# A retention layer fused with an ELU MLP on one core: other queues for the first loads, gated v loads, and a respread unit 3

## The chip, the cores and the metric

The kernel runs on one core of a Trainium2 chip. The metric is the device time of one execution in microseconds (us). The kernel before took 319.91 us (median of five runs, 319.39 to 320.42).

## The reference, cut to what matters

```
scores = (q @ k.T) / sqrt(D)                  # B=8, H=8, S=576, D=64
Dmat   = gamma_h ** (i - j) where i >= j, else 0,  gamma_h = 1 - 2**(-5-h)
x      = (scores * Dmat) @ v                  # heads side by side: 4608 tokens x 512
h      = x @ w_in                             # 512 x 2048
g      = h where h > 0, else exp(min(h, 0)) - 1
out    = g @ w_out                            # 2048 x 512
```

All inputs and the output are float32. The kernel's matrix products are in bfloat16.

## The kernel before

The 4608 tokens are 36 units of 128 rows. The decay is split into a factor for the row and one for the column, so that the retention can go unit by unit with a carried state. For each unit the kernel

- loads v (`load_v`, L79: float32, on SP's queue) and q and k (`load_qk`, L88: on GpSimd's queue, POOL, which casts to bfloat16 on the way),
- multiplies v by the column's decay (`scale_v`, L167, on POOL),
- turns q and k to have the head dimension on the partitions (`turn`, L175: eight PE transposes into PSUM, then one copy on DVE, L189, and one on ACT, L190; from unit 12 on a DMA transpose on SP),
- makes the scores (`scores`, L197), masks them (`masks`, L210, DVE), adds the part of the carried state (`inter`, L221), updates the state (`state`, L237), adds the unit's own part (`intra`, L261), and writes the scaled result to the MLP's input (`put_x`, L273, DVE, with the row's decay `gx`, made on ACT by `make_gx`, L160) and the state (`state_out`, L254, ACT).

The units form groups (0 to 2; 3; 4; 5; 6, 7; and so on up to four). `ffn1` (L316) makes one tile of up to 512 hidden values: four matmuls (L326), e = exp(h) on ACT (L331), m = e - 1 on POOL (L333), and later g = min(max(h, 0), m) on DVE (L310), which also frees the PSUM bank. The DVE instruction is put out three tiles behind by `finish` and `tick` (L306 to L314), sooner where the code calls `finish`. Tiles of group 0 and 1 use three banks of the pool `ps_h` in turn, and every fourth tile the one bank of `ps_m`. `ffn2` and `ffn2_half` make the output tiles.

The order on every engine is the order of the program text (`tc.manual_schedule()`). Each engine works its instructions off in that order, and POOL's DMA issues stand in line with its arithmetic. From L484 on a list of slots with due times sets the order. Before that, for units 0 to 6, it is written out by hand, and that is where the change lies:

- L112 to L114: v of units 0 to 3 on SP, q and k of unit 0 on POOL; then the constants (POOL iotas L131 to L136, DVE, ACT), with q and k of unit 1 at L137.
- L396 to L427: dummy matmuls on zeros (`dummy`, L381), the loads of q and k of units 2 and 3 and of w_in and the first half of w_out, and units 0 to 2 one after the other. Dummies stand between their steps.
- L435 to L450: group 0's 16 FFN1 tiles, with unit 3 between them: v scaled after tile 3; turn, second half of w_out, three dummies, scores and mask after tile 7; the rest (`product`) after tile 11, and then the v loads of units 4 to 9. Of these the first waits for a memset on DVE (the argument `after` of `load_v`).
- L451 to L481: group 1's four tiles, the FFN2 halves of units 0 to 3, and units 4 to 6 between them.

Of the kernel before, what the change touches and what calls it, by code (L numbers as in the profile page):

```python
# [9 lines left out]
FP32 = mybir.dt.float32  # L10
BF16 = mybir.dt.bfloat16
# [6 lines left out]
def kernel(  # L18
# [9 lines left out]
    nc = tc.nc  # L28
    PSUM = bass.MemoryType.PSUM

    B, H, S, D = q.shape
    DM, DF = moe_w_in.shape
    P = 128
# [14 lines left out]
    def place(u):  # L48

        pair, r = divmod(u, R)  # L50
        if r < 4:
            return [(0, 2 * pair, P * r, P)]
        if r == 4:
            return [(0, 2 * pair, 4 * P, 64), (64, 2 * pair + 1, 0, 64)]
        return [(0, 2 * pair + 1, 64 + P * (r - 5), P)]
# [5 lines left out]
    qkpool = ctx.enter_context(tc.tile_pool(name="qkpool", bufs=8))  # L61
# [6 lines left out]
    opool = ctx.enter_context(tc.tile_pool(name="opool", bufs=5))  # L68
# [7 lines left out]

    raws, kns = {}, {}

    def load_v(u, after=None):  # L79

        vv = raw.tile([P, H, D], FP32, name="rv", tag="rv")
        if after is not None:
            after.memset(vv[0:1, 0, 0:1], 0.0)
        for p0, b, s0, n in place(u):
            nc.sync.dma_start(vv[p0 : p0 + n], v[b, :, s0 : s0 + n, :].rearrange("h p d -> p h d"))
        raws[u] = vv

    def load_qk(u, *cs):  # L88

        if u not in kns:  # L90
            kns[u] = qkpool.tile([P, 2, H, D], BF16, name="qkn", tag="qkn")
        for c in cs or (0, 1):
            for p0, b, s0, n in place(u):
                nc.gpsimd.dma_start(  # L94
                    kns[u][p0 : p0 + n, c], (q, k)[c][b, :, s0 : s0 + n, :].rearrange("h p d -> p h d")
                )
# [6 lines left out]
    def load_w_in(n):  # L103
        s = slice(n * 512, (n + 1) * 512)
        nc.gpsimd.dma_start(w_in_sb[:, :, s], w_in_v[:, :, s])

    def load_w_out(c, f0, f1):
        s = (slice(None), slice(f0, f1), slice(c * 256, c * 256 + 256))
        nc.gpsimd.dma_start(w_out_sb[s], w_out_v[s])


    for u in range(4):  # L112
        load_v(u)
    load_qk(0)  # L114

    warm = const.tile([P, 512], BF16, name="warm")
    nc.vector.memset(warm, 0.0)  # L117
# [17 lines left out]
    px_i = xpool.tile([P, 2, S - 64], I32, name="px_i", tag="xt").rearrange("p a b -> p (a b)")[:, :S]  # L135
    nc.gpsimd.iota(px_i, pattern=[[1, S]], base=-MID, channel_multiplier=0)  # L136
    load_qk(1)  # L137

    pk = const.tile([P, R], FP32, name="pk")
    nc.vector.tensor_copy(pk, pk_i)  # L140
# [19 lines left out]
    def make_gx(*hps):  # L160
        for hp in hps:
            nc.scalar.activation(gx[:, hp, :S], px, AF.Exp, bias=bx, scale=lgx[:, hp : hp + 1])
# [4 lines left out]
    def scale_v(u):  # L167
        rv = raws[u]
        n = nat.tile([P, H, D], BF16, name="vn", tag="vn")
        nc.gpsimd.tensor_tensor(  # L170
            n, rv, gk[:, u % R].unsqueeze(2).to_broadcast([P, H, D]), ALU.mult
        )
        vns[u] = n

    def turn(u, bank=None):  # L175

        t = tpool.tile([P, 2, HP, P], BF16, name="qkT", tag="qkT")
        n = kns[u]
        if u < PE_TURNED:
            if bank:  # L180
                pool, tag = bank
                ps = [pool.tile([P, HP, P], BF16, name="tr", tag=tag) for c in range(2)]
            else:
                both = ps_s.tile([P, 2, 2, HP, P], BF16, name="tr", tag="sc")
                ps = [both[:, c, 0] for c in range(2)]
            for c in range(2):
                for hp in range(HP):
                    nc.tensor.transpose(ps[c][:, hp], n[:, c, 2 * hp : 2 * hp + 2].rearrange("p h d -> p (h d)"), ident)  # L188
            nc.vector.tensor_copy(t[:, 0], ps[0])  # L189
            nc.scalar.copy(t[:, 1], ps[1])  # L190
        else:
            nc.sync.dma_start_transpose(
                t.rearrange("p c h t -> p (c h) t"), n.rearrange("p c h d -> p (c h d)")
            )
        qkTs[u] = t
# [14 lines left out]
    def masks(u, i=None):  # L210

        if u not in pts:
            pts[u] = ppool.tile([P, 2, HP, P], BF16, name="pt", tag="pt")
        m = mask[:, 1 if u % R == 4 else 0]
        s = slice(0, 2) if i is None else slice(i, i + 1)
        nc.vector.tensor_tensor(  # L216
            pts[u][:, s].rearrange("p i h t -> p (i h) t"), scs[u][:, s].rearrange("p i h t -> p (i h) t"),
            m.unsqueeze(1).to_broadcast([P, (s.stop - s.start) * HP, P]), ALU.mult,
        )

    def inter(u):  # L221

        o = ps_o.tile([P, HP, P], FP32, name="o", tag="o")
        os_[u] = o
        r = u % R
        if r == 0:
            return
        n = 64 if r == 4 else P
        for hp in range(HP):
            for i in range(2):  # L230
                rows = slice(i * D, (i + 1) * D)
                nc.tensor.matmul(  # L232
                    o[rows, hp, :n], sbs[u][rows, hp], qkTs[u][rows, 0, hp, :n],
                    start=(hp == 0), stop=False, skip_group_check=True,
                )
# [70 lines left out]
    def finish(n=0):  # L306

        while late and late[0][0] <= slot[0] - n:
            _, gt_, ph, m, _ = late.pop(0)
            nc.vector.scalar_tensor_tensor(gt_, ph, 0.0, m, ALU.max, ALU.min)  # L310
# [50 lines left out]
    def ffn2_cols(u, c0, c1, bank, copy, queue):  # L361

        g, it = group_of[u]
        pool, tag = bank
        pm = pool.tile([P, c1 - c0], FP32, name="pmh", tag=tag)
        for ft in range(NFT):
            nc.tensor.matmul(  # L367
                pm, gts[g, ft][:, it * P : (it + 1) * P], w_out_sb[:, ft, c0:c1],
                start=(ft == 0), stop=(ft == NFT - 1),
            )  # L370
        ot = opool.tile([P, c1 - c0], FP32, name="oth", tag="ot")
        copy(ot, pm)
        queue.dma_start(out[u * P : (u + 1) * P, c0:c1], ot)

    def ffn2_half(u, c, bank):
        ffn2_cols(u, c * 256, c * 256 + 256, bank, A if u % 2 else V, nc.scalar)


    V, A, G = nc.vector.tensor_copy, nc.scalar.copy, nc.gpsimd.tensor_copy

    def dummy(n, bank=(ps_m, "pm")):  # L381
        dum = bank[0].tile([P, 512], FP32, name="dum", tag=bank[1])
        for _ in range(n):
            nc.tensor.matmul(dum, warm[:, :P], warm, start=True, stop=True)  # L384

    def product(u):
        inter(u)
        state(u)
        intra(u)
        put_x(u)  # L390
        state_out(u)

    h, m = (ps_h, "ph"), (ps_m, "pm")


    dummy(14)  # L396
    load_qk(2)
    make_gx(0, 1)
    turn(0, h)
    load_w_in(0)  # L400
    scale_v(0)
    load_w_in(1)
    scale_v(1)
    load_qk(3)
    dummy(2)
    for u in range(3):
        scores(u)
        inter(u)
        masks(u)
        if u == 0:  # L410
            make_gx(2, 3)
        if u < 2:
            dummy(3)
            turn(u + 1, h)
        else:
            dummy(4)
        state(u)
        intra(u)
        put_x(u)
        state_out(u)  # L420
        dummy(2)
        if u == 0:
            scale_v(2)
            load_w_in(2)
            load_w_in(3)
            load_w_out(0, 0, 8)
            load_w_out(0, 8, 16)  # L427


    def f1(g, n, bank=None):  # L430
        k = 512 // (P * len(GROUPS[g]))
        ffn1(g, k * n, bank)

    o = (ps_o, "o")
    for n in range(16):  # L435
        f1(0, n, m if n % 4 == 3 else None)
        if n == 3:
            scale_v(3)
        if n == 7:
            turn(3)  # L440
            load_w_out(1, 0, 16)
            finish(1)
            dummy(3, o)
            scores(3)
            masks(3)
        if n == 11:
            product(3)
            load_v(4, nc.vector)
            for u in range(5, 10):
                load_v(u)  # L450
    for n in range(4):  # L451
        f1(1, n, m if n == 3 else None)
        if n == 1:
            load_qk(4)
    finish()
    scale_v(4)
    load_qk(5)
    nc.gpsimd.tensor_copy(gx[:, :, S:], gx[:, :, 0:64])
    for u, bank in enumerate((h, h, h, m)):
        ffn2_half(u, 0, bank)  # L460
    scale_v(5)
    load_qk(6)
    ffn2_half(0, 1, h)
    turn(4)
    ffn2_half(1, 1, h)
    scores(4)
    masks(4)
    scale_v(6)
    load_qk(7)
    ffn2_half(2, 1, h)  # L470
    product(4)
    turn(5)
    ffn2_half(3, 1, m)
    scores(5)
    masks(5)
    load_qk(8)
    f1(2, 0)
    f1(2, 1)
    turn(6)
    f1(2, 2)  # L480
    load_qk(9)  # L481


    slots, start, now = [(f1, 2, 3, 1.0)], {}, 1.0  # L484
    for g in range(3, NG + 1):
# [6 lines left out]
        a, b = 0, 2 if g == 4 else 0  # L492
# [33 lines left out]
    for f, g, s, d in slots:  # L526
        while events and events[0][0] <= now + d / 2:
            _, kind, u = events.pop(0)
# [13 lines left out]
    u = NU - 1  # L542
# [31 lines left out]
```

## Time and profile before

| | |
|---|---|
| median of five runs | 319.91 us |
| the profiled execution | 319.93 us, span 317.8 us |
| PE (TensorE matmul) busy | 307.4 us, 97% |
| POOL busy | 201.7 us, 63% |
| DVE busy | 173.5 us, 55% |
| ACT busy | 130.6 us, 41% |
| TensorE clock granted | 1.00 |
| first FFN1 matmul | 19.33 us after the span's start |
| first FFN1 matmul of group 2 | 53.8 us |

The profile is of one execution. Times are in us from the span's start. PE is TensorE's matmuls, DVE is VectorE, ACT is ScalarE, POOL is GpSimd, SP is SyncE. A name such as `SPq` is the sequencer of that engine, which issues DMAs. A row of the timeline has its start, its length, the engine, the line, the operation, what it writes and reads, how many instructions are merged in it, and in brackets how long the engine stood idle before it and what ended the wait. A row of the chain of waits has its start, its length and what ran; the chain is followed back from the last instruction, at each step to what released it. The time from the issue of a DMA to its landing is a view of its own, and so are the packets of each queue.

### The profile page before, as it was taken

Reading aid. Unit: us, or ns where it says so; the run is one execution under the profiler, and the core shown is the slowest. Engines: PE = TensorE matmul, PEld = TensorE weight load, DVE = VectorE, ACT = ScalarE, POOL = GpSimd, SP = SyncE. Lnnn points to the kernel's source line nnn. Section 1 sums busy time; section 2 is a strip of 40 time slices with the busy share of each in tenths; the row PEclk is TensorE's granted clock in tenths of the full one; section 3 lists DMA queues with packets and bytes.
Section 4 is the critical chain, followed back from the end, with each engine's and each line's share of the span. In section 5 each row is a group of like instructions: output and inputs, shape, how many; then the busy total and the mean of one; then the engine's idle time right before and its main releaser. Section 6 shows DMA issues by size and latency. Waiting matters only on the chain.

```text
span 317.8 us, 7512 instructions
## 1 busy us (share of the span) xinstructions
PE 307.4 (97%) x3011; PEld 173.1 (54%) x3011; DVE 173.5 (55%) x272; ACT 130.6 (41%) x242; POOL 201.7 (63%) x289
## 2 busy tenths in 40 slices
PE   6798999999999999999999999999999999999995
PEld 2455888767766555555444444444444444444444
DVE  4567534658666656665666555555555555434300
ACT  3445512444543544344444444344444444344311
POOL 8956894887987777787777666776664433333300
PEclk9999999999999999999999999999999999999999
DMA  9999999995999999999999999999997200000111
GB/s 145 189 195 194 195 220 215 145 97 39 105 146 174 141 135 169 144 139 163 120 149 134 133 134 134 132 134 134 134 132 85 66 35 36 33 33 34 67 67 67
DMA packets 150195, 39.29 MB, mean 124 GB/s; under 512 B 138640, under 2 KB 146192, under 8 KB 150160
## 3 DMA queue, kind: packets, MB, share of 16 engines
q0 software_dynamic: 81264, 13.64, 56.6%
q1 hardware_dynamic: 66880, 22.88, 38.1%
q10 hardware_dynamic: 2016, 2.29, 2.3%
q8 instruction: 23, 0.38, 0.5%
q14 instruction: 12, 0.10, 0.1%
HBM read 36.70 MB, written 9.44 MB: 145 GB/s over the span
## 4 chain that ended last, share of the span: by engine, by line
PE 88%; DVE 4%; POOL 3%; DMA 2%; issue 1%; ACT 1%; POOLq 0%; DVEq 0%; ACTq 0%
PE ph L326 37%; PE pm L351 33%; PE pmh L367 4%; PE sc L204 4%; PE o L266 3%; PE st L249 2%; PE o L232 2%; DMA qkn<-in_k_dram 2%; POOL qkn L94 2%; PE tr L188 2%; DVE pt L216 1%; DVE xt L279 1%; POOL m L333 1%; PE dum L384 1%; DVE g L310 1%
## 5 line engine op out<-in xcount | busy, mean ns | idle before, releaser
L333 POOL TENSOR_SCALAR m<-e 128x512 bf16<-128x512 f32 (+1 forms) x156 | 90.7, 584 | 98.5 <-ACT e L331 93.2
L326 PE MATMUL ph<-xt,w_in_sb 128*128 128x512 bf16 (+3 forms) x832 | 145.6, 314 | 0.5 <-DVE xt L279 0.2
L310 DVE SCALAR_TENSOR_TENSOR g<-ph,m 128x512 bf16<-128x512 f32 (+1 forms) x156 | 99.8, 647 | 82.7 <-POOL m L333 81.2
L331 ACT ACTIVATE e<-ph 128x512 f32<-128x512 f32 (+1 forms) x156 | 88.0, 564 | 126.5 <-PE ph L326 125.8
L351 PE MATMUL pm<-w_out_sb,g 128*128 128x512 bf16 x496 | 125.5, 379 | 0.0
L326 PEld LDWEIGHTS <-w_in_sb 128*128 128x128 bf16 x832 | 71.5, 98 | 55.3 <-issue 1.4
L351 PEld LDWEIGHTS <-g 128*128 128x128 bf16 x496 | 47.8, 98 | 53.2 <-issue 0.3
L216 DVE TENSOR_TENSOR pt<-sc,mask 128x1024 bf16<-128x1024 f32 x36 | 44.0, 1221 | 20.4 <-PE sc L204 20.2
L170 POOL TENSOR_TENSOR vn<-rv,gk 128x512 bf16<-128x512 f32 x36 | 37.6, 1044 | 0.1
L94 POOL DMA_DIRECT2D qkn<-in_q_dram x40 | 36.0, 900 | 0.8 <-POOLq L558 0.8
L94 POOL DMA_DIRECT2D qkn<-in_k_dram x40 | 34.2, 857 | 0.1
L279 DVE TENSOR_TENSOR xt<-o,gx 128x512 bf16<-128x512 f32 x36 | 24.7, 685 | 15.3 <-PE o L266 15.3
L358 ACT COPY ot<-pm 128x512 f32<-128x512 f32 x31 | 18.1, 585 | 14.3 <-PE pm L351 14.2
L367 PE MATMUL pmh<-w_out_sb,g 128*128 128x256 bf16 (+1 forms) x176 | 18.5, 263 | 0.2 <-DVE g L310 0.2
L258 ACT CAST sb<-st 128x256 bf16<-128x256 f32 x32 | 11.9, 372 | 16.0 <-PE st L249 13.2
L204 PEld LDWEIGHTS <-qkT 64*64 64x64 bf16 x576 | 9.2, 106 | 14.8 <-issue 10.8
L367 PEld LDWEIGHTS <-g 128*128 128x128 bf16 x176 | 15.7, 98 | 2.3 <-issue 0.4
L204 PE MATMUL sc<-qkT 64*64 64x128 bf16 x576 | 15.0, 222 | 1.5 <-ACT qkT L190 1.5
L266 PE MATMUL o<-pt,vn 128*64 128x128 bf16 x288 | 14.3, 221 | 0.0
L232 PE MATMUL o<-qkT,sb 64*64 64x128 bf16 (+1 forms) x256 | 12.3, 214 | 0.0
L190 ACT COPY qkT<-tr 128x512 bf16<-128x512 bf16 x12 | 7.0, 585 | 12.6 <-DVE qkT L189 7.1
L384 PE MATMUL dum<-warm 128*128 128x512 bf16 x35 | 10.9, 443 | 1.2 <-DVE warm L117 1.2
(36 smaller groups left out, 78.8 us busy)
## 6 DMA issues: line engine op xcount, KB each, us to landing
rv<-in_v_dram SPq DMA_DIRECT2D x32, 256.0 KB, 5.6
out_dram<-ot SPq DMA_DIRECT2D x27, 256.0 KB, 2.3
qkn<-in_q_dram POOLq DMA_DIRECT2D x32, 128.0 KB, 5.1
qkn<-in_k_dram POOLq DMA_DIRECT2D x32, 128.0 KB, 4.5
w_in_sb<-in_moe_w_in_dram POOLq DMA_DIRECT2D x4, 512.0 KB, 8.1
out_dram<-oth ACTq DMA_DIRECT2D x9, 128.0 KB, 5.8
w_out_sb<-in_moe_w_out_dram POOLq DMA_DIRECT2D x2, 512.0 KB, 12.5
w_out_sb<-in_moe_w_out_dram POOLq DMA_DIRECT2D x1, 1024.0 KB, 11.1
```

The costliest lines, as they stand in the source:

```text
L94: nc.gpsimd.dma_start(kns[u][p0 : p0 + n, c], (q, k)[c][b, :, s0 : s0 + n, :].rearrange("h p d -> p h d"))
L170: nc.gpsimd.tensor_tensor(n, rv, gk[:, u % R].unsqueeze(2).to_broadcast([P, H, D]), ALU.mult)
L204: nc.tensor.matmul(sc[j * 64 : (j + 1) * 64, i, hp], t[r, 1, hp, j * 64 : (j + 1) * 64], t[r, 0, hp], start=(hp == 0), stop=(hp == HP - 1) ...
L216: nc.vector.tensor_tensor(pts[u][:, s].rearrange("p i h t -> p (i h) t"), scs[u][:, s].rearrange("p i h t -> p (i h) t"), m.unsqueeze(1).t ...
L266: nc.tensor.matmul(o[i * D : (i + 1) * D, hp], vns[u][:, h], pts[u][:, i, hp], start=(u % R == 0 and hp == 0), stop=(hp == HP - 1), skip_g ...
L279: nc.vector.tensor_tensor(xts[g][:, :, i * P : (i + 1) * P], os_[u], gx[:, :, s0 : s0 + P], ALU.mult)
L310: nc.vector.scalar_tensor_tensor(gt_, ph, 0.0, m, ALU.max, ALU.min)
L326: nc.tensor.matmul(ph[:, i * n : (i + 1) * n], w_in_sb[:, j, f : f + P], xts[g][:, j, :n], start=(j == 0), stop=(j == KJ - 1), skip_group_ ...
L331: nc.scalar.activation(e[:, w], ph[:, w], AF.Exp)
L333: nc.gpsimd.tensor_scalar(m[:, w], e[:, w], -1.0, 1.0, ALU.add, ALU.mult)
L351: nc.tensor.matmul(pm, gts[g, ft][:, it * P : (it + 1) * P], w_out_sb[:, ft], start=(ft == 0), stop=(ft == NFT - 1))
L367: nc.tensor.matmul(pm, gts[g, ft][:, it * P : (it + 1) * P], w_out_sb[:, ft, c0:c1], start=(ft == 0), stop=(ft == NFT - 1),)
```

## The change

Five things are done, all in the part written out by hand.

1. q and k of unit 0 come first on SP's queue, as float32 into two buffers of the pool for output tiles. ACT casts q to bfloat16, DVE casts k. v of units 0 to 2 follow on SP. v of unit 3 moves to POOL's queue, after q and k of unit 3.
2. POOL makes its iotas before its first DMA. After them it issues q and k of units 1 and 2 and the first part of w_in, all before the first `scale_v`. The other weights follow `scale_v(2)`, ahead of the loop over units 0 to 2.
3. `make_gx` is done for one pair of heads before unit 0's turn and for three after its mask. There are 12 dummies at the start instead of 14, and 8 after unit 1 instead of 2.
4. In group 0's FFN1, v of unit 3 is scaled after tile 6 instead of 3. The mask of unit 3 is made in two halves (after tile 7 and after tile 8 in the program; on DVE they stand one behind the other), `product(3)` comes after tile 10 instead of 11, and the second half of w_out is issued after tile 11 instead of 7.
5. The v loads of units 4 to 9 are no longer issued together after tile 11. Each stands at a later place beside the q/k load of its unit, and each waits for a one-element memset on DVE.

```diff
+    kns[0] = qkpool.tile([P, 2, H, D], BF16, name="qkn", tag="qkn")
+    raw0 = [opool.tile([P, H, D], FP32, name="rqk", tag="ot") for c in range(2)]
+    for c in range(2):
+        nc.sync.dma_start(raw0[c], (q, k)[c][0, :, 0:P, :].rearrange("h p d -> p h d"))
-    for u in range(4):
+    for u in range(3):
         load_v(u)
-    load_qk(0)
...
     load_qk(1)
+    load_qk(2)
+    load_w_in(0)
...
-    dummy(14)
-    load_qk(2)
-    make_gx(0, 1)
+    dummy(12)
+    A(kns[0][:, 0], raw0[0])
+    V(kns[0][:, 1], raw0[1])
+    make_gx(0)
     turn(0, h)
-    load_w_in(0)
     scale_v(0)
     load_w_in(1)
     scale_v(1)
     load_qk(3)
+    load_v(3, queue=nc.gpsimd)
+    scale_v(2)
+    load_w_in(2)
+    load_w_in(3)
+    load_w_out(0, 0, 8)
+    load_w_out(0, 8, 16)
     dummy(2)
     for u in range(3):
...
         if u == 0:
-            make_gx(2, 3)
+            make_gx(1, 2, 3)
...
-        dummy(2)
-        if u == 0:
-            scale_v(2)
-            load_w_in(2)
-            load_w_in(3)
-            load_w_out(0, 0, 8)
-            load_w_out(0, 8, 16)
+        dummy((2, 8, 2)[u])
...
     for n in range(16):
         f1(0, n, m if n % 4 == 3 else None)
-        if n == 3:
+        if n == 6:
             scale_v(3)
         if n == 7:
             turn(3)
-            load_w_out(1, 0, 16)
             finish(1)
             dummy(3, o)
             scores(3)
-            masks(3)
+            masks(3, 0)
+        if n == 8:
+            masks(3, 1)
+        if n == 10:
+            product(3)
         if n == 11:
-            product(3)
-            load_v(4, nc.vector)
-            for u in range(5, 10):
-                load_v(u)
+            load_w_out(1, 0, 16)
     for n in range(4):
         f1(1, n, m if n == 3 else None)
+        if n == 0:
+            load_v(4, nc.vector)
         if n == 1:
             load_qk(4)
     finish()
+    load_qk(5)
+    load_v(5, nc.vector)
     scale_v(4)
-    load_qk(5)
     nc.gpsimd.tensor_copy(gx[:, :, S:], gx[:, :, 0:64])
     for u, bank in enumerate((h, h, h, m)):
         ffn2_half(u, 0, bank)
+    load_qk(6)
+    load_v(6, nc.vector)
     scale_v(5)
-    load_qk(6)
     ffn2_half(0, 1, h)
     turn(4)
+    load_qk(7)
+    load_v(7, nc.vector)
     ffn2_half(1, 1, h)
     scores(4)
     masks(4)
     scale_v(6)
-    load_qk(7)
     ffn2_half(2, 1, h)
     product(4)
     turn(5)
+    load_qk(8)
+    load_v(8, nc.vector)
     ffn2_half(3, 1, m)
     scores(5)
     masks(5)
-    load_qk(8)
     f1(2, 0)
     f1(2, 1)
     turn(6)
     f1(2, 2)
     load_qk(9)
+    load_v(9, nc.vector)
```

`load_v` gets an argument for its queue, which is SP's if it isn't given.

More of the change, by code (lines that the diff above doesn't have):

```diff
@@ L77, with load_v @@
     raws, kns = {}, {}
-    def load_v(u, after=None):
+    def load_v(u, after=None, queue=nc.sync):
         vv = raw.tile([P, H, D], FP32, name="rv", tag="rv")
@@ L84, in load_v @@
         for p0, b, s0, n in place(u):
-            nc.sync.dma_start(vv[p0 : p0 + n], v[b, :, s0 : s0 + n, :].rearrange("h p d -> p h d"))
+            queue.dma_start(vv[p0 : p0 + n], v[b, :, s0 : s0 + n, :].rearrange("h p d -> p h d"))
         raws[u] = vv
```

## The prediction

> **What bounds the kernel now.** I read the busy table and the 40 slices first. The profiled execution took 319.93 us, its span is 317.8, so 2.1 us lie around the span; the median of the five runs shown is 319.91, so the sum below can be made against either.
>
> ```profile
> PE 307.4 (97%) x3011; PEld 173.1 (54%) x3011; DVE 173.5 (55%) x272; ACT 130.6 (41%) x242; POOL 201.7 (63%) x289
> ...
> PE   6798999999999999999999999999999999999995
> ...
> DMA  9999999995999999999999999999997200000111
> ```
>
> TensorE (PE) is full except in the first two slices (16 us) and the last. All edits of the change lie in the first 60 us, so what it is worth is by how much it moves the PE's work there. What follows moves with it unchanged. Next, the chain of work that ended last, in order of time (start, length, what), for 0 to 60 us:
>
> ```profile
> 5.50 6.54 DMA qkn<-in_k_dram
> 12.04 0.05 issue
> 12.09 0.40 PE tr L188 x4
> ...
> 15.90 0.54 PE dum L384 x2
> 16.44 0.35 PE sc L204 x16
> ...
> 19.33 2.12 PE ph L326 x12
> ...
> 24.73 1.03 DVE g L310 x2
> 25.76 0.34 DVE qkT L189
> 26.10 0.02 issue
> 26.12 0.59 ACT qkT L190
> 26.71 0.04 issue
> 26.76 0.42 PE sc L204 x16
> ```
>
> Three facts. First, the start waits for k of unit 1 (k1): issued on GpSimd (POOL) at 5.50, landed at 12.04. From its transposes to the first FFN1 matmul, 12.09 to 19.33, the chain hardly leaves the PE: 7.24 us, of which DVE's 0.70 (put_x of unit 2) is the only piece off it. Second, dummy matmuls lie in that chain. Third, within FFN1 the turn of unit 3 costs a bubble: its scores start only at 26.76, because DVE does two g operations (to 25.76) ahead of the copy of qkT. Then the timeline:
>
> ```profile
> 1.27 1.08 POOL L94 DMA_DIRECT2D qkn<-in_q_dram  x1 [0.82 <-POOLq L558]
> ...
> 23.17 1.04 POOL L170 TENSOR_TENSOR vn<-rv,gk 128x512 bf16<-128x512 f32 x1
> ...
> 26.06 1.22 POOL L109 DMA_DIRECT2D w_out_sb<-in_moe_w_out_dram  x1
> ...
> 32.12 1.16 POOL L333 TENSOR_SCALAR m<-e 128x384 bf16<-128x384 f32 x2 [1.06 <-ACT e L331]
> ...
> 32.66 2.53 DVE L310 SCALAR_TENSOR_TENSOR g<-ph,m 128x384 bf16<-128x384 f32 x4 [0.29 <-POOL m L333]
> ```
>
> The last column is the idle time before and what ended it. POOL's scaling of v3 at 23.17 pushes back m of tile 4 and so the two g ahead of qkT. The issue of the second half of w_out (26.06, 1.22 us) falls into the bubble. The m of tile 12 is free to start when its e is there (32.12); its g ends at 33.21, just as the PE wants that PSUM bank for the first tile of group 1 (three ph banks, so that tile reuses tile 12's).
>
> **What the Trainium skill says.** "DMA: Bandwidth & Descriptors", section "SWDGE vs HWDGE vs iDMA": a cast during a DMA is tied to GpSimd's software queue (SWDGE); a load from SP is plain. That is why SP's q0 and k0 need a float32 stage and two casts. The trace before has every q/k load on POOL. Same page, "Queues, rings and completion order": each DMA engine goes round-robin between the queues that have work. The trace agrees: the v loads landed at 4.0, 6.2, 8.1 and 10.2 us, the first alone and the rest 2 us apart beside the q/k loads. Same page, "Issuing engines are not separate DMA queues": issuing from several engines saves only issue time. Here the packet records give about 540 packets per 0.5 us for SP alone, 600 for POOL alone and 480 for both, so sharing buys no rate. "TensorE: Matmul & The Clock Gate", "Back-to-back issue gap": N/2.4 + 2.5 ns warm, 216 ns at N = 512. The chain's dummies agree: three took 0.75 us, four 0.97.
>
> **The change, part by part.**
>
> *Start.* Each q, k or v load of 128 rows is 1,024 packets. Before: SP had four v loads (first packets at 1.7, SP alone until 3.9), POOL issued q0, k0, then 1.2 us of iotas, then q1, k1. The first software packet came at 3.9, 2.65 us after its issue; k0's 1,024 were moved by 7.6 and it landed 1.5 later, at 9.15. After: SP carries q0, k0, v0, v1, v2; POOL does iotas first, then q1, k1, q2, k2, w_in0. The iotas can start at 0.9 to 1.3, so q1 is issued at 2.1 to 2.5, in q0's old place but 0.8 to 1.2 us later. SP has a little less left beside it (some 1,900 packets against 2,240), so I take q0/k0's old course shifted: first packet 4.7 to 5.1, k1 landed at 9.95 to 10.35. A later pair of loads (issued 36.55, first packets 37.85) had only 1.3 us of latency; with that, k1 would land near 9.0, but then q2/k2, sharing for longer, would land near 12.7 and hold turn(2). Upper bound: 10.8, if SP's loads get an equal share (1.12 us per load for each queue's turn). I take k1 at 10.1: 1.95 us earlier than 12.04.
>
> Is anything later than that? q0 lands at 4.0 (as v0 did), k0 near 5.1. Casts: ACT about 0.58 (its 128x512 f32 copies take 0.585), DVE about 0.45 (px, 128x576, 0.46). DVE's constants are through 2 us earlier, near 4.8, since POOL's iotas are. Two dummies fewer end by 5.7; turn(0), scores(0) near 6.9 instead of 10.3. So unit 0 is ready long ahead of k1 and these casts cost nothing; without that cover they would add 0.6. make_gx(1,2,3), 3 x 0.81 us on ACT, ends near 9.2, ahead of k1's copy. v0, v1, v2 land near 6.0, 8.2, 10.4; vn of unit 2 is ready near 13.7, needed near 17. w_in0 (512 packets of 1,024 B, 2.56 us) follows k2 and lands near 14.5, w_in1 near 17; both before they are needed. So the 7.24 us of PE chain follow k1, plus the new dummies after unit 1: 8 instead of 2, 6 x 0.216 = 1.30 us. They stand after turn(2), ahead of scores(2), whose operands were ready about 0.3 us before the old two ended: nothing covers them. Start of FFN1: 19.33 - 1.95 + 1.30 = 18.7, a gain of 0.65; bounds 18.1 (early first packet; k2 holds) and 19.4 (k1 at 10.8).
>
> *FFN1, unit 3.* With v3 scaled after tile 6 instead of 3, g of tile 5 ends near 25.15 instead of 25.76 (before's clock), when the transposes end (25.13): scores(3) move from 26.76 to about 26.25, a gain of 0.5. The mask in two halves is about 0.65 + 0.65 on DVE against 1.22; product(3) now comes three tiles after the scores, so it waits for nothing. The price: w_out's second half is issued after m of tile 11. POOL does nothing else for 1.22 us, and queued behind it is m of tile 12. Formerly product(3) stood between tiles 11 and 12 and gave POOL 0.85 us of air; now it stands before tile 11. Tiles follow every 0.65 us, m takes 0.52, so the air is 0.13: m12 is 1.22 - 0.13 = 1.09 late, its g too, and the PE waits for that bank before group 1. Slack was 0.04 (33.21 against 33.25): a stall of 1.05. Bounds: 0, if bank and DVE leave air that I don't see, and 1.3. Net for this part +0.55 (-0.5 to +0.8).
>
> *Later.* Nearly the same POOL order (m, m, four q4/k4 issues of 0.69 each, m, m); the 0.23 us wait for the bank ahead of unit 2's FFN2 half takes up perhaps 0.1. v3's own load, now on POOL behind q3/k3, costs 0.9 us of POOL's time near 12 and lands near 20, needed near 24. v4 to v9 each wait for a DVE memset of 0.06 us placed among the group 1 and FFN2 work. SP queues the following v loads behind each; who waits is scale_v on POOL, and behind scale_v(5) and (6) are the q7, k7, q8, k8 issues and then m of group 2 at 55.67. v5 can be issued near 41.4 and land near 46 to 47, where POOL stood at 43.64: up to 3 us later, against 4.65 us that POOL idled ahead of 55.67. Hidden; with that cover gone it would cost its excess, up to 1 us. Fewer v packets beside w_out and q4/k4 help transfers that arrived in time anyway: 0.
>
> Sum: 319.93 - 0.65 + 0.55 - 0.1 = 319.7.
>
> **The rivals.** (A) The forecast, the two large terms cancel: 319.7, own range 319.1 to 320.3. (B) The w_out issue costs the PE nothing, because m12 has air or the issue overlaps: 319.7 - 1.05 = 318.65; with the early first software packet 318.1. For it: in the old run POOL's issue at 26.06 delayed nobody. Against it: at 36.61 the chain has POOL's issues on the path (m after them at 39.30, the PE released at 40.73). (C) Slower: the dummies outweigh the earlier k1. Place: between o of unit 1 and scores(2); price 1.30 whatever the loads do. With the stall of 1.05 and 0.5 of bubble it decides against the change from k1 later than 10.3 (12.04 - 1.75), and by over 0.64 from later than 10.9: k1 at 11.0 gives 319.93 - 1.04 + 1.30 + 0.45 = 320.65. For it: the round-robin, now against five SP loads. Against: SP has two loads through before POOL begins. (D) v5 or v6 lands after 50, POOL reaches group 2's m late: 319.7 + 1.2 = 320.9.
>
> **How the numbers follow.** A measurement of this kernel tells about 0.2% (0.64 us) from no change. A has 0.40, of which 0.08 lie below 319.27; B 0.34; C 0.18; D 0.08. Faster 0.42, same 0.32, slower 0.26. The range 318.3 to 320.9 takes in A, most of B, C and the near half of D. A's own is 319.1 to 320.3; cases of both signs are open.
>
> **What would show it.** k1's landing near 10.1 and FFN1's first matmul near 18.7; eight dummies of 0.216 back to back before scores(2), with qkT of unit 2 done before they end; scores(3) 6.9 us after FFN1's start instead of 7.43; POOL's w_out issue directly ahead of m12, and a PE wait of about 1 us, ended by g, ahead of group 1; POOL idle still ahead of group 2's first m. It is wrong if w_in0 or k2 sets FFN1's start, if the PE's clock falls in the idle stretch before k1 lands, or if the PE runs from tile 15 into group 1 with no wait.

## The result and the profile after

The changed kernel takes 318.99 us (median of 38 runs, 318.46 to 320.48), the kernel before 320.18 beside it (75 runs): the ratio is 0.9963, 95% interval 0.9954 to 0.9972. It is faster by 0.37%. The forecast case was "no difference", at 319.7 us with its own range of 319.1 to 320.3; the time lies just under that, between the forecast and the faster rival (B), and in the whole range (318.3 to 320.9). The five runs from which the prediction started had a median of 319.91, the 75 here 320.18, and the later batches 320.27 to 320.36; why that is so belongs to the result and comes below.

The profiled execution of after took 318.72 us (before: 319.93), with a span of 316.9 (317.8). The busy table of after and its row of slices for the PE:

```profile
PE 308.0 (97%) x3015; PEld 173.6 (55%) x3015; DVE 172.7 (55%) x279; ACT 131.2 (41%) x243; POOL 200.7 (63%) x288
...
PE   7899899999999999999999999999999999999995
```

The PE's first two slices (0 to 16 us) are a digit fuller each, 6 and 7 became 7 and 8; the fourth (24 to 32 us) rose from 8 to 9, and the fifth (32 to 40) fell from 9 to 8. So the change gains at the start, gains in unit 3's turn and loses something just after. The chain of work that ended last tells what; here is that of after from 3 to 31 us (start, length, what):

```profile
3.07 6.69 DMA qkn<-in_k_dram
...
9.81 0.40 PE tr L193 x4
...
13.62 1.83 PE dum L389 x8
...
18.33 2.12 PE ph L331 x12
...
24.17 0.44 DVE qkT L194
...
24.63 0.59 ACT qkT L195
...
25.27 0.42 PE sc L209 x16
...
30.43 0.17 POOL w_out_sb L109
```

Read it against the chain of before. k of unit 1 lands at 9.76 (3.07 + 6.69) instead of 12.04 and still sets the start. The eight dummies are in the chain, 1.83 us with no gap around them. FFN1's first matmul comes at 18.33 instead of 19.33. One g instead of two stands ahead of the copy of qkT, and the scores of unit 3 come 6.94 us after FFN1's start instead of 7.43. Then the chain goes where it did not go before: over POOL's issue of w_out's second half. The timeline of after shows what follows (start, length, engine, line, operation, and in brackets the idle time before it and what ended it):

```profile
30.43 1.22 POOL L109 DMA_DIRECT2D w_out_sb<-in_moe_w_out_dram  x1
...
31.68 1.94 POOL L338 TENSOR_SCALAR m<-e 128x384 bf16<-128x384 f32 x4
...
32.24 1.98 DVE L315 SCALAR_TENSOR_TENSOR g<-ph,m 128x384 bf16<-128x384 f32 x4 [1.16 <-POOL m L338]
32.85 1.33 PE L331 MATMUL ph<-xt,w_in_sb 128*128 128x128 bf16 x21 [0.91 <-DVE g L315]
```

The issue holds POOL for 1.22 us, m of tile 12 stands behind it, its g behind that, and the PE waits 0.91 us for the bank: the stall of the prediction, with the chain of causes that it named.

Milestones of the two profiled executions, after minus before: FFN1's first matmul -1.00; e of tile 8 -1.49; first tile of group 1 -0.42; the last output copies, 280 us later, -0.45. So in this pair the PE's order is settled by 33 us and nothing later gives or takes more than a few hundredths. The pair differs by 1.21 us in all: 0.44 in this order; 0.41 in the tail from the last store's issue to the end of the span (2.84 against 3.25, while the landing of that store takes the same 1.6); 0.35 in the time around the span (1.81 against 2.16). The last two rows of the timeline, first of before, then of after:

```profile
314.20 0.29 DVE L372 COPY oth<-pmh 128x128 f32<-128x128 f32 x1 [1.42 <-PE pmh L367]
314.52 0.33 SPq L373 DMA_DIRECT2D out_dram<-oth  x1
```

```profile
313.76 0.29 DVE L377 COPY oth<-pmh 128x128 f32<-128x128 f32 x1 [1.42 <-PE pmh L372]
314.08 0.33 SPq L378 DMA_DIRECT2D out_dram<-oth  x1
```

The record of each execution gives its mean granted TensorE clock. Below, an execution is called low when this mean is 0.995 or less, and at full clock when it is 0.997 or more; none lies between. Before was low in 58 of the 109 executions recorded beside the experiments (median 320.55, the others 319.75), after in 4 of 61 (the others 318.97). At full clock the change is thus worth 0.78 us, and the other 0.4 us of the 1.19 are the executions in which before lost its clock. The ratios below leave out executions that took over 1.5% more than the fastest of their kernel, which are three of "Start alone".

Where the 0.78 us lie is not what the profiled pair suggests. From FFN1's first matmul to the last output copy, kernels with the same FFN1 order and no long wait take the same time in every profile: 294.86 to 294.88 us in five with before's order (before: 314.20 - 19.33), 295.43 to 295.46 us in four with after's (after: 313.76 - 18.33). What differs between executions at full clock is when FFN1 starts. Take this stretch, the tail with the 0.32 us from the last copy to the last store, and the time around the span from the full-clock medians, and an estimate of FFN1's start is left: 19.16 us for before, 18.61 for after. By it the start gains 0.55 us, not the 1.00 of the pair; unit 3's new place costs 0.56; and the PE's order as a whole gains nothing. What is left is the tail, 0.41, and the time around the span, 0.37: it is 2.15 us for before and 1.78 for after in the median, and no execution of after has more than 1.84 or of before less than 2.09. What makes these two shorter is not shown.

### The profile page after: what moved, and what is told of

Its sections match the earlier page's. It is cut to its first block, busy times and chain, and to the rows that moved or that the text cites. A ratio compares the mean times of both kernels' runs of the same rounds, so it can differ in the third digit from the quotient of the medians.

```text
span 316.9 us, 7528 instructions
## 1 busy us (share of the span) xinstructions
PE 308.0 (97%) x3015; PEld 173.6 (55%) x3015; DVE 172.7 (55%) x279; ACT 131.2 (41%) x243; POOL 200.7 (63%) x288
## 4 chain that ended last, share of the span: by engine, by line
PE 88%; DVE 4%; POOL 3%; DMA 2%; issue 1%; ACT 1%; POOLq 0%; DVEq 0%; ACTq 0%
PE ph L331 37%; PE pm L356 33%; PE pmh L372 5%; PE sc L209 4%; PE o L271 3%; PE st L254 2%; PE o L237 2%; DMA qkn<-in_k_dram 2%; PE tr L193 2%; DVE pt L221 1%; PE dum L389 1%; POOL m L338 1%; DVE g L315 1%; DVE xt L284 1%; POOL qkn L94 1%
## 5 line engine op out<-in xcount | busy, mean ns | idle before, releaser
L221 DVE TENSOR_TENSOR pt<-sc,mask 128x1024 bf16<-128x1024 f32 (+1 forms) x37 | 44.0, 1191 | 20.5 <-PE sc L209 20.3
L94 POOL DMA_DIRECT2D qkn<-in_q_dram x39 | 35.0, 898 | 0.0
L94 POOL DMA_DIRECT2D qkn<-in_k_dram x39 | 33.3, 856 | 0.1
L195 ACT COPY qkT<-tr 128x512 bf16<-128x512 bf16 x12 | 7.0, 585 | 10.6 <-PE tr L193 4.0
```

The costliest lines, as they stand in the source:

```text
L94: nc.gpsimd.dma_start(kns[u][p0 : p0 + n, c], (q, k)[c][b, :, s0 : s0 + n, :].rearrange("h p d -> p h d"))
L221: nc.vector.tensor_tensor(pts[u][:, s].rearrange("p i h t -> p (i h) t"), scs[u][:, s].rearrange("p i h t -> p (i h) t"), m.unsqueeze(1).t ...
```

## The experiments

All kernels compute the whole reference. Each batch had its own runs of before beside it: 320.36 (35 runs) in the first, 320.28 (26) in the second, 320.27 (48) in the third. The second batch ran on another chip than the first and third; before was low there in 13 of 26 executions, on the first chip in 45 of 83. The theory going in was the prediction's: two large terms, the start and the w_out stall, that nearly cancel, and v loads that don't matter. The first batch takes the change apart into its three pieces; the second tests the two terms by undoing each inside the changed kernel; the third goes after what the first two left over.

### Start alone

The changed loads, casts and dummies at the start; FFN1's order and all later v loads as before. Against after:

```diff
-        if n == 6:
+        if n == 3:
             scale_v(3)
         if n == 7:
             turn(3)
+            load_w_out(1, 0, 16)
...
-            masks(3, 0)
...
+            masks(3)
         if n == 11:
+            product(3)
+            load_v(4, nc.vector)
+            for u in range(5, 10):
+                load_v(u)
```

> The kernel before with the change's new start alone (loads over two queues, casts, order of the weights, 12 and 8 dummies); unit 3's place and the v loads as before. Theory 1 (the PE's order alone sets the time): k1 lands near 9.8, the first FFN1 matmul comes near 18.3 instead of 19.3, unit 3's bubble stays, no wait ahead of group 1, and all later PE work is 1.0 us earlier: about 319.1 against 320.1. Theory 2 (transfers that land late hold a part back): with the v loads of units 4 to 9 issued together, the last load of k of unit 4 lands near 45 as before, the turn of unit 4 wants it 1.0 us earlier, and only 0.3 to 0.7 us of the gain are left after 46 us, with a wait for that load in the trace.

Measured: 322.09 us (14 runs), ratio 1.0038 (1.0008 to 1.0068). Slower, which none of the theories had; but its seven executions at full clock go from 318.80 to 321.24, so the loss is not in all of them. In the profiled one (321.19) FFN1 starts at 18.28 and everything stays about 1.04 ahead of before up to 46 us; then 2.66 are lost. The timeline of ACT in this kernel:

```profile
47.31 0.37 ACT L377 COPY oth<-pmh 128x256 f32<-128x256 f32 x1 [0.70 <-PE pmh L372]
47.71 6.42 ACTq L378 DMA_DIRECT2D out_dram<-oth  x2
54.17 0.37 ACT L263 CAST sb<-st 128x256 bf16<-128x256 f32 x1 [6.49 <-DMA out_dram<-oth]
```

Two stores, 0.34 us each to issue, take 6.42 us from the first's start to the second's end, where the same two take 2.67 in before. The second gets away at 53.79; a v load, issued at 43.46, landed at 53.72. In the trace the record of a DMA's issue names the semaphore that tells of its landing, and this store and this v load have the same one. Behind the store in ACT's queue stand the cast of the state and unit 5's copy of qkT, and the PE's weight loads wait 2.9 us for that qkT. The trace ends 1.6 us behind that of before.

### FFN1 part alone

The start and the v loads as before. Against before:

```diff
-        if n == 3:
+        if n == 6:
             scale_v(3)
         if n == 7:
             turn(3)
-            load_w_out(1, 0, 16)
...
-            masks(3)
+            masks(3, 0)
+        if n == 8:
+            masks(3, 1)
+        if n == 10:
             product(3)
...
+        if n == 11:
+            load_w_out(1, 0, 16)
```

> The kernel before with the change's new place of unit 3 inside group 0's FFN1 alone (v scaled after tile 6, mask in halves, product after tile 10, second half of w_out issued after tile 11). Theory 1: scores of unit 3 start 6.9 us after FFN1's start instead of 7.4, but a wait of about 0.9 us ahead of group 1 ends with g of tile 12: net about +0.5 us. Theory 2: the second half of w_out and the loads of unit 4 behind it in the same queue land later beside the ungated v loads, so more than that: +0.7 to +2 us, with a wait for w_out or unit 4's k.

Measured: 335.61 us (6 runs), ratio 1.0477 (1.0452 to 1.0501): 15 us slower, where half a microsecond was expected. The part itself does what was said (scores of unit 3 earlier, 0.9 us of wait ahead of group 1). The loss lies between 40 and 66 us. The waits of that stretch in this kernel (who waited for what: total us, times, longest):

```profile
ACT qkT L190 <- DMA out_dram<-oth: 11.0, 1, 11.0
...
PE sc L204 <- ACT qkT L190: 6.4, 1, 6.4
```

It is the same picture, worse: three of ACT's stores are issued at 50.18, 55.36 and 61.58; v loads landed at 50.10, 55.28 and 61.20, and each of the stores has the semaphore of the v load that landed before it. For the last of them the chain of waits goes from ACT's queue straight back to the v load:

```profile
50.35 10.85 DMA rv<-in_v_dram
...
61.22 0.02 ACTq L373
```

Meanwhile the last of q4/k4, which landed at 44.99 in before, landed at 52.0, the PE waits 0.9 us for w_out's second half, now issued just ahead of the six v loads, and, short of work, the PE runs at a granted clock of 0.67 in 46 to 60 us.

### Gating alone

The v loads of units 4 to 9 moved behind memsets and placed as in after; the rest as before:

```diff
             product(3)
-            load_v(4, nc.vector)
-            for u in range(5, 10):
-                load_v(u)
...
+        if n == 0:
+            load_v(4, nc.vector)
...
+    load_v(5, nc.vector)
     scale_v(4)
```

> The kernel before with the later, gated v loads of units 4 to 9 alone (and the q/k loads of units 5 to 9 at the places that go with them). Theory 1: no PE wait between 31 and 60 us was set by these loads, so 0 within 0.1 us of the trace and no change of the time. Theory 2: the change's median is 1.2 us lower while its trace is only 0.44 us earlier from 35 us to the last copy, so a part of the gain lies in executions in which the old kernel waits for a late load; then this kernel's median is 0.4 to 0.8 us lower than before, though its profile's PE order is the same.

Measured: 319.55 us (14 runs), ratio 0.9991 (0.9976 to 1.0007); at full clock 319.40 against before's 319.75. Over all executions the gate by itself is worth nothing that can be told from zero. The 0.35 at full clock are not its work: by the estimate above these nine executions started FFN1 at 18.84 instead of 19.16, ahead of the first line that the gate touches. Its profiled execution started FFN1 late, at 21.07, because the clock fell: see the next run.

### The kernel before, once more

No edit.

> The kernel before, unchanged, for what two medians of one kernel differ by and how much the trace's start and tail move from execution to execution. Theory 1: the first FFN1 matmul comes within 0.3 us of 19.33 and the turn of unit 4 follows with no wait. Theory 2: in some executions k of unit 4 lands after 46 us and the PE waits for it.

Measured: 320.47 us (14 runs), ratio 0.9998 (0.9980 to 1.0016). The use of this run is its profile. The windows of 2 us in it (busy time and count for each engine, then the granted clock):

```profile
6.00:8.00 2.00, 0.96 (x7) 0.29 (x5) 1.12 (x3) 0.96 (x2) 2.00 (x3) 1.00 1.78 193
8.00:10.00 2.00, 0.54 (x5) 0.55 (x6) 0.05 (x1) 0.00 (x0) 2.00 (x4) 0.76 2.11 186
10.00:12.00 2.00, 2.00 (x21) 0.70 (x20) 0.46 (x1) 1.90 (x3) 1.98 (x3) 0.50 2.35 161
```

The third figure of a row is the PE, the third from the end its clock: 0.96 us of work in 6 to 8, 0.54 in 8 to 10, then "2.00 busy" at half clock, with 21 matmuls, where the profiled execution of before that the prediction used has 24 in 1.44 us at full clock. FFN1 starts at 20.02 instead of 19.33. The same kernel, the same order, 0.7 us later. A thin stretch alone does not decide it: that other execution was as thin and kept its clock:

```profile
6.00:8.00 2.00, 0.53 (x5) 0.23 (x4) 0.75 (x2) 0.97 (x2) 2.00 (x3) 1.00 1.71 188
8.00:10.00 2.00, 0.84 (x7) 0.34 (x6) 0.42 (x1) 0.35 (x1) 2.00 (x4) 1.00 2.14 185
```

### The changed kernel, once more

No edit to after.

> The changed kernel, unchanged, beside the three that follow. Theory 1 (the PE's order alone): the trace's first FFN1 matmul within 0.1 us of 18.33, the time 0.44 us below before's where both run at full granted clock. Theory 3 (the old start leaves the PE idle for so long before k1 that its clock drops in about half of the executions, the new one doesn't): hardly any execution with a mean granted clock under 0.996, where the old kernel had 27 of 49, and so a median about 1.2 us below before.

Measured: 318.96 us (21 runs), ratio 0.9960 (0.9950 to 0.9970). In this profile k of unit 2, not of unit 1, holds the start: issued at 4.81, it lands at 13.33, and FFN1 starts at 18.95, 0.62 later than in the first profile of the same kernel. One of the 21 was low. The wait ahead of group 1 is again 0.9.

### Two dummies after unit 1 again

Against after:

```diff
-        dummy((2, 8, 2)[u])
+        dummy(2)
```

> The changed kernel with 2 dummies after unit 1 instead of 8. If these six matmuls are plain cost on the PE's path (6 x 0.216 us), FFN1 starts near 17.05 and all later PE work, time too, is 1.3 us earlier: about 317.7. If they cover a wait (w_in's first part landed at 15.2, the second at 17.7, wanted 2.6 us after FFN1's start; unit 4's k at 43.7, wanted at 45.7), less than that, with the wait in the trace. If they are there for the PE's clock, the granted clock falls in more executions and the median moves by less than 1 us.

Measured: 318.01 us (5 runs), ratio 0.9928 (0.9913 to 0.9942); that is 0.98 less than after, and the trace is 0.96 ahead from FFN1 on. The chain of this kernel:

```profile
13.93 0.54 PE dum L389 x2
14.47 0.35 PE sc L209 x16
...
17.36 2.12 PE ph L331 x12
```

1.83 became 0.54: 1.29, as priced. k1 landed 0.31 later in this execution (10.07), and 1.29 - 0.31 = 0.98. In this trace nothing covers the dummies, and leaving them out let no clock fall (no low execution of 5). The medians differ by 0.98 as well; whether the missing 0.3 is chance can't be told from five executions, with FFN1's start moving by up to 1.2 us between profiles of after's start.

### w_out's second half issued early

Against after: the issue back at tile 7, in the bubble of unit 3's turn; everything else as in after.

```diff
         if n == 7:
             turn(3)
+            load_w_out(1, 0, 16)
...
-        if n == 11:
-            load_w_out(1, 0, 16)
```

> The changed kernel with the second half of w_out issued after unit 3's turn (after tile 7), as before. If its issue on GpSimd ahead of m of tile 12 makes the PE's 0.9 us wait ahead of group 1, that wait goes, scores of unit 3 stay at 6.9 us after FFN1's start, and all later work is 0.9 us earlier: about 318.1. Rival: the issue now delays m of tile 7 or 8, and with it g and the mask of unit 3, so that half of it or more comes back ahead of product of unit 3.

Measured: 318.44 us (6 runs), ratio 0.9944 (0.9924 to 0.9965), about 0.5 less than after. Its profiled execution began badly (k2 landed at 13.90, FFN1 at 19.52, 1.19 after that of after), yet at the first tile of group 1 it is only 0.12 behind: 1.07 won between, and no wait ahead of group 1. From FFN1's first matmul to the last copy the kernel takes 294.38 us instead of 295.43. The median shows half of that: by the estimate its five executions at full clock started FFN1 at 19.0, some 0.4 later than those of after, and the sixth was low.

### Both

The last two edits together.

> Both: 2 dummies after unit 1 and the early issue of w_out's second half. If both are plain cost, the gains add: 2.2 us below the changed kernel, about 316.8. Rival: transfers then hold it: unit 4's k, landed 2.0 us ahead of its turn in the changed kernel, or a store's issue on ACT that waits for a v load with the same semaphore, so that 1.0 us or more of the 2.2 comes back between 40 and 60 us.

Measured: 316.89 us (4 runs), ratio 0.9895 (0.9878 to 0.9912), none low: the fastest kernel of the study, 3.3 us below before and 2.1 below after. Its chain:

```profile
13.72 0.54 PE dum L389 x2
...
17.14 2.12 PE ph L331 x12
```

The trace is 2.24 ahead of after: 1.19 at FFN1's start, 1.05 more at group 1, where the PE no longer waits. The two terms add; on top of the two dummies the early issue is worth 318.01 - 316.89 = 1.12 in the medians.

### Start and gate

After, with FFN1's order as before (the first half of the diff of "start alone", v loads left gated).

> The changed kernel with unit 3 inside FFN1 as before (v scaled after tile 3, w_out's second half after tile 7, product after tile 11): the new start and the gated v loads together. If the 2.66 us that the new start alone lost between 46 and 60 us came from ACT's store issues standing behind ungated v loads, that loss is gone: FFN1 at 18.3 to 18.9, no PE wait over 0.6 us between 40 and 60 us, the time 1.0 us below before's at full clock and about 1.4 in the median, so about 318.9. If the loss came from the new start itself (v3 or the weights landing later), it stays, and the time is near 321.

Measured: 319.10 us (19 runs), ratio 0.9975 (0.9959 to 0.9990). The gate takes away what the start alone had lost: 319.10 against 322.09, at full clock 318.51 against 320.79. In its trace the two stores that took 6.42 us take 2.65, as in before, and no wait of the PE in 40 to 60 us is over 0.6. Against gating alone the start is worth 318.51 - 319.40 = -0.89 at full clock; of this the tail is 0.38 (2.83 against 3.21) and the time around the span 0.24 (1.92 against 2.16), which leaves about 0.3 for FFN1's start. Nine of 19 executions were low, though, with a median of 320.17, 1.66 above the others; the profiled one was not, so no trace shows where.

### FFN1 part and gate

After, with the start as before.

> The kernel before with unit 3's new place and the gated v loads, the start as before. If the v loads in front of w_out's second half and of ACT's stores made the 16 us of loss of unit 3's new place alone, what is left is its own price: 0.5 us earlier scores, 0.9 us of wait ahead of group 1, about +0.5 us on before: near 320.7 in the median. If the place itself costs, several us remain.

Measured: 320.48 us (14 runs), ratio 0.9996 (0.9978 to 1.0014); at full clock 319.79, which is 0.39 above gating alone. The gate saves 15 us against "FFN1 part alone". In the trace FFN1 starts 0.30 before that of before and group 1 is 0.27 behind: the part costs 0.57. The medians hide some of it, because the time around the span is 0.37 shorter than with the gate alone (1.79 against 2.16). Eight of 14 were low: the start is the old one.

### Before, with six more dummies at the front

Against before, to see whether an empty PE makes the clock fall:

```diff
-    dummy(14)
+    dummy(20)
```

> The kernel before with 20 instead of 14 dummies at the start. They end near 7.5, before q of unit 0 lands at 7.6, so that no step of the PE is later and its first idle stretch of 1.5 us is filled. Theory 3 (the PE's clock falls after the idle stretches of the old start in about half of the executions): executions with a mean granted clock under 0.996 become rare, and the median falls by 0.4 to 0.6 us to about 319.75. Rival (the clock's phase is set by chance, or by the stretches from 8 to 11 us): their share stays about a half and the median within 0.2 us of before's.

Measured: 319.78 us (22 runs), ratio 0.9989 (0.9978 to 0.9999), and 1 low execution of 22, against 58 of 109 without them. The windows of this kernel:

```profile
6.00:8.00 2.00, 1.59 (x11) 0.70 (x9) 1.11 (x3) 0.96 (x2) 2.00 (x3) 1.00 1.75 192
8.00:10.00 2.00, 1.11 (x22) 0.59 (x22) 0.05 (x1) 0.92 (x2) 2.00 (x4) 1.00 2.23 172
```

PE 1.59 and 1.11 us in 6 to 10, where before has 0.53 and 0.84, and the clock stays at 1.00. The median equals before's full-clock median (319.75).

### No dummies after units 0 and 1

On top of the fastest version, the dummies after unit 0 and unit 1 left out (two after unit 2 kept):

```diff
-        dummy((2, 8, 2)[u])
+        if u == 2:
+            dummy(2)
```

> The early issue of w_out's second half, and no dummies after units 0 and 1 at all (2 after unit 2). Against the version with 2 after each unit: scores of units 1 and 2 then wait for their qkT on ACT and start 0.2 to 0.35 us earlier each, about 0.5 us in all: near 316.4. Rival: the PE's clock falls in the idle stretches that come with it, and the time is the same or longer.

Measured: 317.65 us (6 runs), ratio 0.9910 (0.9887 to 0.9933): 0.8 slower than with two each, with less work. Five of 6 executions were low. (The version with two each ran on the other chip; before's median was 320.28 there and 320.27 here.) Its windows:

```profile
10.00:12.00 2.00, 1.55 (x44) 1.13 (x41) 1.23 (x2) 0.86 (x2) 2.00 (x4) 0.84 1.76 174
12.00:14.00 2.00, 2.00 (x13) 1.10 (x11) 0.59 (x1) 0.00 (x0) 2.00 (x3) 0.50 1.27 206
```

Half clock in 12 to 14. The one full-clock execution took 316.88, no less than the fastest version; one execution can't show whether the expected 0.5 is there when the clock holds. With the clock counted in, the two dummies per unit earn their place; eight after unit 1 do not.

## Why the prediction was right in its terms and short of what it did not count

**The start, put at -0.65: -1.00 in the profiled pair, about -0.55 by the medians.** Mechanism as predicted: k1 sets it, the 7.24 us of PE chain follow, and the dummies come on top uncovered (1.29 us for six). k1 landed at 9.76 where 10.1 was taken; in the other profiles with the new start it came between 9.72 and 10.55. Before's k1 moves as well, 12.04 in its profile and 11.33 in that with 20 dummies. So the pair joined an early execution of after to a late one of before, and FFN1's start at 18.7, as forecast, is nearer to the estimate (18.61) than the 18.33 of the profile. Between the two kernels with the gate and the old FFN1 order the start comes out smaller, at about -0.3, so its size is known to some 0.3 only. One of the prediction's own signs of being wrong did come: in two of the profiles k2 holds the start, with FFN1 at 18.95 and 19.52, the latter beyond the bound of 19.4. DVE's cast of k0 took 0.75 instead of 0.45, covered as was said.

**The bubble, put at -0.5: it was -0.49** (6.94 against 7.43 us from FFN1's start to the scores). **The stall, put at +1.05: 0.91 as a wait of the PE, 1.05 to 1.07 when undone.** Net for the FFN1 part +0.55 predicted; +0.58 in the trace of after (-1.00 became -0.42) and +0.57 in that of the part with the gate. The full-clock medians show +0.39 (part with gate against gate) and +0.46 (after against start with gate, 318.97 against 318.51), because the time around the span shortens with this part.

**Later, put at -0.1: -0.02.** By the estimate the PE's order thus gains nothing, -0.55 + 0.56, against the -0.2 that was predicted. The two large terms cancel, as forecast.

**What carried it past "no difference" was in none of the terms.** Of the 1.19 us about 0.4 are the clock, 0.41 the tail and 0.37 the time around the span. The prediction took the 2.1 us around the span, and all that follows the first 60 us, to stay as they were, and gave no reason for it. The time fell into the range only because rival B had stretched the range downwards; B itself, in which the issue costs the PE nothing, falls (0.91 us of wait). That is luck.

The clock: the prediction names a fall of the PE's clock before k1 lands as a thing that would make it wrong, but as a danger of the changed kernel; it was the kernel before that had it, in half of its executions, and the one profile shown had none. That filling the thin stretch cures the old start is shown (six dummies more, 1 low execution of 22). The Trainium skill, "TensorE: Matmul & The Clock Gate", section "What's actually happening", lets the clock fall to half after at least one idle window of some 3.4 us; here it fell after a longest gap of 1.87 us, with the PE busy for 0.96 us of 6 to 8 and 0.54 of 8 to 10. The measurement decides: a stretch that is only thin can be enough. It is not always so, since the profiled execution of before was as thin and kept its clock, and what decides between the two is not shown.

The two ends: the tail is 2.83 to 2.85 us in the seven profiled kernels that have both the new start and the gate, and 3.20 to 3.27 in the seven others. Near its end SP works off a row of waits, with a gap of 0.4 between two of them; before the change the gap lies behind the landing of the last store, after it ahead of that landing, which fits the difference but was not tested. The time around the span is 1.71 to 1.85 us in every execution of the kernels with unit 3's new place, 1.82 to 1.97 in those with the new start and the old place, and 2.08 to 2.23 in those with neither. So it goes with the program and not with the execution; nothing in the traces says why.

**The gate, put at 0: right as a step, wrong as a judgement.** Alone it is worth nothing that can be measured. But the other two parts without it lose 2.66 us and 15 us. The prediction said that the v loads help transfers "that arrived in time anyway". It looked for who waits for v, and for q/k and w_out; it did not ask what else waits when a v load is late. ACT's output stores did: in the two kernels four stores were issued 0.07 to 0.38 us after an unrelated v load had landed, each of them with the semaphore of that very v load, and with the gate the long ones of these waits are gone. Before, with the same ungated loads, escapes narrowly: its store at 51.10 shares its semaphore with a v load that landed at 51.02. With the gate the v load that shares a semaphore with a store of this stretch has landed at least 2.3 us ahead of it (46.02 for the store at 48.33 in after). No run changed the semaphores alone.

**Rivals C and D.** C's point of decision, k1 later than 10.3, was passed in one profile only (about 10.6). D (v5 or v6 late) did not come: v5, issued at 40.89, landed at 46.02, POOL went on at 46.19 after a copy on DVE, and it still stood idle for 3.43 us ahead of group 2's first m.

Left open: why "start and gate" loses its clock in 9 of 19 executions and "start alone" in 7 of 14, while after, with the same start, does so in 4 of 61. So the new start alone is not the cure. Their low executions cost 1.66 and about 2.7 us, those of before 0.8, so the clock seems to fall at another place than in before; the profiled executions had full clock, and no trace shows it. The two kernels were run on the first chip, and the second runs of after on the other; before was equally often low on both, but no run of after's order with its eight dummies is known to be of the first chip, so that the chip plays a part isn't ruled out. ("FFN1 part and gate", low in 8 of 14, has the old start.)

## What to carry to other kernels

Price a change on the chain of work, but take the base from many executions and look at their granted clock: 0.8 us lost in half of the runs is invisible in one good profile and larger than most edits. Do the same for the gain: two profiles gave the start 1.00 us, the medians 0.3 to 0.55. The spans of all executions tell how much of a difference lies outside the span, 0.37 us of 0.78 here. Dummy matmuls are worth just as many as keep the clock up; the six further ones on the path cost 1.29 us, 0.215 each, and a DMA issue of 1.22 us on an engine that also computes cost 1.06. A part that is worth nothing alone can be what lets the others pay: try the parts alone and in pairs before leaving one out.

## What the runs showed of the hardware that was not expected

- An engine's DMA issue can stand for a transfer that is not its own: two stores on ACT took 6.42 us instead of 2.67, and went on 0.07 us after a v load, issued on another queue with the same semaphore, had landed.
- The PE's clock fell to 0.5 in 10 to 12 us after thin work (1.5 us of 4), without a gap of 2 us; low executions of before took 0.8 us longer. In the new start, two dummies after each of two units (0.54 us each in the chain) stand between 0 low executions of 4 and 5 of 6.
- k1, the second load that POOL issues in the new start, took 6.6 to 7.5 us from its issue to its landing beside SP's loads, and k2, two loads behind it, landed at 12.63, 13.33 and 13.90: the start of such a kernel spreads by over 1 us between executions (FFN1 at 18.33, 18.95 and 19.52 with identical code up to there).
